# A pruned-weight matmul: PSUM banks shared by two tiles, and the first weights loaded in two parts

## The chip, the cores and the metric

One core of a Trainium2 chip. The metric is the device time of one execution in microseconds (us); lower is better. A timed execution is some 1.8 us longer than the span in its profile.

## The reference, cut to what matters

```python
B, S, D = 16, 512, 1024                       # x [16,512,1024], w [1024,1024], b [1024], all bf16
wg = w.reshape(D // 4, 4, D)                  # groups of four rows
mag = jnp.abs(wg)
thr = second largest of mag along axis 1
wp = (wg * (mag >= thr)).reshape(D, D)        # 2:4 pruning
return jnp.einsum("bsd,df->bsf", x, wp) + b
```

So: 8192 rows of x against a 1024 x 1024 matrix that must first be pruned, in groups of four rows. The matmul is nearly all of the time; what can be lost is the time until pruned weights and transposed x are there.

## The kernel before

The rows of w are laid out so that a partition holds the four rows of a group side by side. w is pruned in **pieces**: 0 to 3 are columns 0-256, 256-512, 512-768 and 768-1024 of the first half of the rows, 4 and 5 are the second half in 512 columns. While VectorE prunes, TensorE works on the first eight **tiles** of x (128 rows each): it transposes them, and multiplies each piece as soon as it is ready ("M6.0y" is tile 6, piece 0, the last two rows of each group). The sums lie in six PSUM banks; ScalarE evicts them ("S"), and GpSimd adds the bias later.

```python
load_w(0, 0, 256)               # SyncE's queue: piece 0, 256 KB
load_x(7, 8, "act")             # ScalarE's queue: x of tile 7
load_x(5, 7)                    # SyncE again: x of tiles 5 and 6, and so on
load_x(0, 2)
load_w(0, 256, 512)             # piece 1
load_x(2, 4)
load_x(4, 5)
load_w(0, 512, 1024)            # pieces 2 and 3, 512 KB
# ... (cut)
def mm_piece(t, i, ms):         # one tile, one piece
    g, c0, c1 = pieces[i]
    h = c0 // FH                # FH = 512: a bank holds ONE tile, two pieces
    # ... (cut)
order = {                       # each engine's instructions in program order (cut)
  "pe":  "T7a F2 T5a T6a F6 T0a T1a F6 M6.0x M5.0x ... M3.1y M2.2 M4.2 ...",
  "dve": "abs0 lo0 hi0 t20 t10 thr0 mask0x mult0x mask0y abs1 mult0y ... thr2 lo3 mask2 mult2 ...",
  "act": "C7a C5a C6a C0a C1a C2a C4a abs2 abs3 S6h0 C3a S5h0 ...",
}
```

T is a transpose, C its copy to SBUF, F a filler matmul on zeros that keeps TensorE busy while it has no data.

Of the kernel before, what the change touches and what calls it, by code (L numbers as in the profile page):

```python
# [10 lines left out]
def kernel(  # L11
# [7 lines left out]
    nc = tc.nc  # L19
    P = 128  # L20
# [12 lines left out]
    FH = 512  # L33
# [6 lines left out]
    NPK = 8  # L40
    LEAD = 4
    GROUPS = ((0, 5), (5, 8))
    LATE = 8
    sizes = (4, 8, 8, 8, 8, 8, 8)
    batches = []
    t0 = NPK + LEAD
# [29 lines left out]
    def act(i):  # L76
        return seq("act", i)
# [20 lines left out]
    def issue(eng, out_, in_):  # L98
        q = nc.sync if eng == "sp" else nc.scalar
        return seq(eng, q.dma_start(out_, in_))  # L100

    def load_w(g, c0, c1, eng="sp"):
        issue(eng, w_sb[:, g, :, c0:c1], wv[:, g, :, c0:c1])

    def load_x(ta, tb, eng="sp"):
        xs = const.tile([P, tb - ta, HK], bf16, name=f"x_{ta}")
# [2 lines left out]
        for t in range(ta, tb):  # L109
            x_sb[t] = xs[:, t - ta, :]  # L110

    load_w(0, 0, 256)
    load_x(7, 8, "act")
    act(nc.scalar.activation(spark[:], zeros[:, :1], Act.Abs))
    load_x(5, 7)
    load_x(0, 2)
    load_w(0, 256, 512)
    load_x(2, 4)
    load_x(4, 5)
    load_w(0, 512, 1024)  # L120
    load_w(1, 0, 512)
    sp(nc.sync.dma_start(bias_sb[:], b.partition_broadcast(P)))
# [19 lines left out]
    class Piece:  # L142
# [12 lines left out]
        def abs_act(self):  # L155
            act(nc.scalar.activation(self.mag[:], self.w, Act.Abs))  # L156

        def do(self, step, ms):
            magv = self.mag[:].rearrange("p (a j) f -> p a j f", j=2)
            hi, lo, thr = self.hi, self.lo, self.hi[:, 0, :]  # L160
            n = ms.stop - ms.start
            if step == "abs":
                dve(nc.vector.tensor_single_scalar(  # L163
                    self.mag[:].bitcast(u16), self.w.bitcast(u16), 0x7FFF, op=Alu.bitwise_and))
            elif step == "hi":
                self.tt(hi[:], magv[:, :, 0, :], magv[:, :, 1, :], Alu.max)
            elif step == "lo":
                self.tt(lo[:], magv[:, :, 0, :], magv[:, :, 1, :], Alu.min)
            elif step == "t1":
                self.tt(hi[:, 0, :], hi[:, 0, :], hi[:, 1, :], Alu.min)  # L170
            elif step == "t2":
                self.tt(lo[:, 0, :], lo[:, 0, :], lo[:, 1, :], Alu.max)
            elif step == "thr":
                self.tt(thr, hi[:, 0, :], lo[:, 0, :], Alu.max)
            elif step == "mask":
                self.tt(self.mag[:, ms, :], self.mag[:, ms, :],
                        thr[:, None, :].to_broadcast([P, n, self.n]), Alu.is_ge)
            else:
                self.tt(wp[:, self.g, ms, self.c0:self.c1], self.w[:, ms, :], self.mag[:, ms, :], Alu.mult)
# [14 lines left out]
        xpk[t] = xt  # L194

    ps_open = {}
    part = {"": slice(0, 4), "x": slice(0, 2), "y": slice(2, 4)}
    left = {}

    def mm_piece(t, i, ms):  # L200
        g, c0, c1 = pieces[i]
        h = c0 // FH
        new = (t, h) not in ps_open
        if new:
            ps_open[(t, h)] = psum_o.tile([P, FH], fp32, name="ps")
            left[(t, h)] = sum(4 for pc in pieces if pc[0] == 0 and pc[1] // FH == h)
        ps = ps_open[(t, h)]
        for m in range(ms.start, ms.stop):
            left[(t, h)] -= 1
            pe(nc.tensor.matmul(ps[:, c0 - h * FH:c1 - h * FH], lhsT=xpk[t][:, m, :],  # L210
                                rhs=wp[:, g, m, c0:c1],
                                start=(new and m == ms.start), stop=(left[(t, h)] == 0),
                                skip_group_check=True))

    xlead = const.tile([P, KT, LEAD * P], bf16)
# [27 lines left out]

    staged = {}

    def stage(t, h):
        st = stg.tile([P, FH], fp32, name=f"st{h}")
        act(nc.scalar.copy(st[:], ps_open.pop((t, h))[:]))  # L248
        staged[(t, h)] = st

    order = {
        "pe": (
            "T7a F2 T5a T6a F6 T0a T1a F6 M6.0x M5.0x M0.0x M7.0x M1.0x M1.0y M6.0y M5.0y T2a M0.0y "
            "T4a M7.0y T3a M2.0x M2.0y M6.1y M5.1y M2.1y M7.1y M0.1x M6.1x M5.1x M1.1y M0.1y M2.1x "
            "M7.1x M1.1x M4.0x M4.1x M4.0y M4.1y M3.0x M3.1x M3.0y M3.1y M2.2 M4.2 M7.2 M6.2 M3.2 "
            "M1.2 M2.3 M6.3 M7.3 M3.3 M5.2 M4.3 A3h0 M1.3 M0.3 A2h0 A3h1 A1h0 M0.2 M5.3 A0h0 A1h1 "
            "A2h1 A0h1"
        ),
        "dve": (
            "abs0 lo0 hi0 t20 t10 thr0 mask0x mult0x mask0y abs1 mult0y hi1 lo1 t11 t21 thr1 mask1y "  # L260
            "mult1y mask1x mult1x lo2 hi2 t22 t12 thr2 lo3 mask2 mult2 hi3 t13 t23 thr3 mask3 mult3 "
            "abs4 hi4 lo4 t14 t24 thr4 mask4 mult4 abs5 hi5 lo5 t25 t15 thr5 mask5 mult5"
        ),
        "act": (
            "C7a C5a C6a C0a C1a C2a C4a abs2 abs3 S6h0 C3a S5h0 S0h0 S7h0 S1h0 S2h0 S4h0 S3h0 S2h1 "
            "S6h1 S7h1 S4h1 S1h1 S3h1 S0h1 S5h1"
        ),
        "sp": (
            "W0.0 X0 W0.1 X1 W1.0 Y1 W1.1 Y0"
# [3 lines left out]
    p = {}  # L273
    halves = {0: ('x', 'y'), 1: ('x', 'y')}

    def all_of(tok, i):
        return [tok + x for x in halves.get(i, ("",))]

    def split_tok(tok):
        k = tok[-1] if tok[-1] in "xy" else ""  # L280
        return (tok[:-1] if k else tok), k

    transposed = []
# [1 line left out]
    def needs(eng, tok):  # L285
        base, k = split_tok(tok)
        if tok[0] == "C":
            return ["T" + tok[1:]]
        if tok[0] == "T":
            return ["C" + transposed[-2]] if len(transposed) > 1 else []  # L290
        if tok[0] == "F":
            return []
        if tok[0] == "W":
            g, h = map(int, tok[1:].split("."))
            return [n for i, pc in enumerate(pieces) if pc[0] == g and pc[1] // FH == h for n in all_of(f"mult{i}", i)]
        if tok[0] in "XY":
            return []
        if tok[0] == "A":
            return ["X0", f"W0.{tok.split('h')[1]}"]
        if base[0] == "M":  # L300
            t, i = base[1:].split(".")
            return [f"C{t}a", f"mult{i}{k}"]
        if tok[0] == "S":
            t, h = tok[1:].split("h")
            return [f"M{t}.{n}" for i, pc in enumerate(pieces) if pc[0] == 0 and pc[1] // FH == int(h)
                    for n in all_of(str(i), i)]
        i, step = base[-1], base[:-1]
        before = {"abs": [], "hi": ["abs"], "lo": ["abs"], "t1": ["hi"], "t2": ["lo"],
                  "thr": ["t1", "t2"], "mask": ["thr", "hi", "lo"], "mult": ["mask"]}[step]
        return [b_ + i + (k if b_ == "mask" else "") for b_ in before]  # L310

    def emit(eng, tok):
        base, k = split_tok(tok)
        if tok[0] == "T":
            transpose(int(tok[1:-1]))
            transposed.append(tok[1:])
        elif tok[0] == "F":
            filler(int(tok[1:]))
        elif tok[0] == "W":
            g, h = map(int, tok[1:].split("."))  # L320
            spread(g, h * FH, (h + 1) * FH)
        elif tok[0] == "X":
            xnat.update(load_lead(int(tok[1:])))
        elif tok[0] == "Y":
            xnat.update(load_low(int(tok[1:])))
        elif tok[0] == "A":
            open_nat(*map(int, tok[1:].split("h")))
        elif tok[0] == "C":
            copy_xt(int(tok[1:-1]))
        elif tok[0] == "M":  # L330
            mm_piece(*map(int, base[1:].split(".")), part[k])
        elif tok[0] == "S":
            stage(*map(int, tok[1:].split("h")))
        else:
            i = int(base[-1])
            if i not in p:
                p[i] = Piece(i)
            if eng == "act":
                p[i].abs_act()
            else:  # L340
                p[i].do(base[:-1], part[k])

    def run(queues):
        while any(queues.values()):
# [24 lines left out]

    pruned = const.tile([P, 1], bf16)  # L370
    pool(nc.gpsimd.tensor_copy(out=pruned[:], in_=wp[:, 1, 3, Dout - 1:]))
    closes = [(8, 0), (9, 0), (10, 0), (11, 0), (5, 0), (6, 0), (7, 0), (8, 1), (9, 1), (10, 1), (11, 1), (5, 1), (6, 1), (7, 1), (0, 0), (0, 1), (1, 0), (1, 1), (2, 0), (2, 1), (3, 0), (3, 1), (4, 0), (4, 1)]
    for t, h in closes:
        if t < NPK:
            pool(nc.gpsimd.tensor_tensor(staged[(t, h)][:], staged[(t, h)][:], bias_sb[:, h * FH:(h + 1) * FH], op=Alu.add))  # L375

    def evac(o, ps, c0, c1, add=None):
        dve(nc.vector.tensor_tensor(o[:, c0:c1], ps, bias_sb[:, c0:c1] if add is None else add, op=Alu.add))  # L378

    def rows(t):  # L380
        if t < NPK:
# [10 lines left out]
    def close(t, h):  # L392
# [3 lines left out]
        if ps is None:  # L396
            ps = psum_o.tile([P, FH], fp32, name="ps")
        nat(xnat[t], ps[:], h * FH, (h + 1) * FH, 4, 8, first=4 if t < NPK else 0, koff=4 if t < NPK else 0)
        add = staged.pop((t, h))[:] if t < NPK else None
        evac(outs[t], ps[:], h * FH, (h + 1) * FH, add)  # L400
        closed[t] = closed.get(t, 0) + 1
        if closed[t] == 2:
# [61 lines left out]
```

## Time and profile before

| | before |
|---|---|
| median of the first three runs | 233.93 us (233.49 to 234.32) |
| the profiled execution | 234.54 us, span 232.7 us |
| first matmul of piece 0 | 7.08 us |
| TensorE waits for an eviction | 0.71 us, until 13.89 |
| first matmul of piece 2 | 15.62 us |
| last bias add on VectorE starts | 230.11 us |

The table is read against TensorE, which is 98% busy: a gain is real only if TensorE reaches its last, unbroken stretch earlier. The lines are shown in the prediction below.

### The profile page before, as it was taken

What the parts mean: (1) busy time and instruction counts of PE and PEld (TensorE: products, weight loads), DVE (VectorE), ACT (ScalarE), POOL (GpSimd) and SP (SyncE); (2) the same over time, 40 slices, a digit from 0 to 9 for tenths busy, and PEclk for the clock granted to TensorE, in tenths of its full rate; (3) what the DMA queues carried; (4) which work ended last, traced back from release to release, by engine and by line L of the source; (5) the groups of instructions that cost most, each with busy time, mean ns of one, the idle gap of its engine ahead of it and who ended that gap; (6) DMA issues with size and microseconds to landing.
All of it is one profiled execution on the core that took longest, in us unless ns stands there. A gap on an engine that the chain in (4) does not pass through costs nothing.

```text
span 232.7 us, 2873 instructions
## 1 busy us (share of the span) xinstructions
PE 227.9 (98%) x1164; PEld 112.5 (48%) x1164; DVE 107.5 (46%) x181; ACT 14.4 (6%) x28; POOL 18.7 (8%) x23
## 2 busy tenths in 40 slices
PE   8989999999999999999999999999999999999995
PEld 4877544554444444444444444444444444444443
DVE  3889968763244244234334334324324424423434
ACT  4395200000000000000000000000000000000000
POOL 1000099910000000000000000000000000000000
PEclk9999999999999999999999999999999999999999
DMA  6996989998489611992239921696228951122122
GB/s 192 337 222 143 171 186 172 367 303 255 187 177 218 195 64 71 217 267 105 90 91 221 274 93 45 139 251 197 93 90 165 252 172 65 70 90 90 49 89 90
DMA packets 78652, 38.19 MB, mean 164 GB/s; under 512 B 63664, under 2 KB 71344, under 8 KB 78640
## 3 DMA queue, kind: packets, MB, share of 16 engines
q1 hardware_dynamic: 68128, 21.27, 46.0%
q10 hardware_dynamic: 10512, 16.75, 20.0%
q8 instruction: 9, 0.15, 0.3%
q14 instruction: 3, 0.02, 0.1%
HBM read 3.41 MB, written 16.78 MB: 87 GB/s over the span
## 4 chain that ended last, share of the span: by engine, by line
PE 93%; DMA 3%; SPq 1%; ACT 1%; issue 0%; DVE 0%
PE ps L233 88%; PE ps L210 4%; DMA w_sb<-in_w_dram 3%; PE tp L233 1%; SPq L100 1%; ACT mag L156 1%; ACT st L248 0%; DVE o L378 0%
## 5 line engine op out<-in xcount | busy, mean ns | idle before, releaser
L233 PE MATMUL ps<-wp_nat,xb 128*128 128x512 bf16 (+2 forms) x848 | 179.8, 375 | 0.0
L233 PEld LDWEIGHTS <-xb 128*128 128x128 bf16 x848 | 82.4, 98 | 97.5
L378 DVE TENSOR_TENSOR o<-ps,bias_sb 128x512 bf16<-128x512 f32 (+1 forms) x112 | 71.6, 677 | 113.6 <-PE ps L233 113.5
L375 POOL TENSOR_TENSOR st<-st,bias_sb 128x512 f32<-128x512 f32 x16 | 17.9, 1158 | 0.0
L210 PE MATMUL ps<-wp,xt 128*128 128x256 bf16 x128 | 15.2, 272 | 0.7 <-ACT st L248 0.7
L233 PE MATMUL ps<-wp_nat,xlow 128*128 128x512 bf16 x64 | 14.1, 379 | 0.0
L210 PEld LDWEIGHTS <-xt 128*128 128x128 bf16 x128 | 12.2, 98 | 2.8 <-issue 0.9
L378 DVE TENSOR_TENSOR o<-ps,st 128x512 bf16<-128x512 f32 x16 | 11.1, 692 | 2.9 <-PE ps L233 2.7
L233 PE MATMUL ps<-wp_nat,xlead 128*128 128x512 bf16 x48 | 11.0, 379 | 0.0
L233 PEld LDWEIGHTS <-xlow 128*128 128x128 bf16 x64 | 7.2, 112 | 6.7
L233 PEld LDWEIGHTS <-xlead 128*128 128x128 bf16 x64 | 6.3, 98 | 6.9
L248 ACT COPY st<-ps 128x512 f32<-128x512 f32 x16 | 8.4, 605 | 5.1 <-PE ps L210 5.1
L132 PE MATMUL ps<-zeros 128*128 128x128 bf16 (+1 forms) x28 | 4.8, 331 | 1.0 <-DVE zeros L86 1.0
L153 DVE TENSOR_TENSOR wp<-w_sb,mag 128x512 bf16<-128x512 bf16 (+2 forms) x8 | 5.5, 691 | 0.2
L153 DVE TENSOR_TENSOR mag<-mag,hi 128x512 bf16<-128x512 bf16 (+2 forms) x8 | 5.5, 689 | 0.2
L233 PE MATMUL tp<-wp_nat,xlead 128*128 128x512 bf16 x16 | 4.1, 379 | 0.0
L132 PEld LDWEIGHTS <-zeros 128*128 128x128 bf16 x28 | 2.6, 120 | 2.7 <-issue 1.7
L153 DVE TENSOR_TENSOR lo<-mag 128x512 bf16<-128x512 bf16 (+1 forms) x6 | 3.1, 510 | 1.3 <-ACT mag L156 1.3
L163 DVE TENSOR_SCALAR mag<-w_sb 128x1024 uint16<-128x1024 uint16 (+1 forms) x4 | 2.2, 556 | 3.1 <-DMA w_sb<-in_w_dram 3.1
L188 PE MATMUL tp<-ident,x 128*128 128x128 bf16 x32 | 2.9, 220 | 0.5 <-DMA x<-in_x_dram 0.3
L193 ACT COPY xt<-tp 128x256 f32<-128x256 f32 x8 | 2.8, 374 | 5.0 <-PE tp L188 4.7
L153 DVE TENSOR_TENSOR hi<-mag 128x512 bf16<-128x512 bf16 (+1 forms) x6 | 3.1, 509 | 0.1
(16 smaller groups left out, 14.4 us busy)
## 6 DMA issues: line engine op xcount, KB each, us to landing
out_dram<-o ACTq DMA_DIRECT2D x56, 256.0 KB, 2.7
wp_nat<-wp SPq DMA_DIRECT2D x16, 128.0 KB, 2.8
out_dram<-o ACTq DMA_DIRECT2D x14, 128.0 KB, 1.7
w_sb<-in_w_dram SPq DMA_DIRECT2D x3, 512.0 KB, 7.8
x<-in_x_dram SPq DMA_DIRECT2D x3, 256.0 KB, 4.1
w_sb<-in_w_dram SPq DMA_DIRECT2D x2, 256.0 KB, 3.8
bias_sb<-in_b_dram SPq DMA_DIRECT2D x1, 256.0 KB, 7.8
x<-in_x_dram ACTq DMA_DIRECT2D x1, 128.0 KB, 2.3
```

Source lines behind the costliest of these rows:

```text
L100: return seq(eng, q.dma_start(out_, in_))
L132: pe(nc.tensor.matmul(warm_ps[:, :rep * P], lhsT=zeros[:], rhs=zeros[:, None, :].to_broadcast([P, rep, P]), start=True, stop=True))
L153: dve(nc.vector.tensor_tensor(out, a, b_, op=op))
L156: act(nc.scalar.activation(self.mag[:], self.w, Act.Abs))
L163: dve(nc.vector.tensor_single_scalar(self.mag[:].bitcast(u16), self.w.bitcast(u16), 0x7FFF, op=Alu.bitwise_and))
L188: pe(nc.tensor.transpose(tp[:, m, :], xg[:, m, :], ident[:]))
L193: act(nc.scalar.copy(xt[:].bitcast(fp32), xpk[t].bitcast(fp32)))
L210: pe(nc.tensor.matmul(ps[:, c0 - h * FH:c1 - h * FH], lhsT=xpk[t][:, m, :], rhs=wp[:, g, m, c0:c1], start=(new and m == ms.start), stop=(l ...
L233: pe(nc.tensor.matmul(ps, lhsT=xt[:, kt - koff, :], rhs=wp_nat[:, kt, c0:c1], start=(kt == first), stop=(kt == last)))
L248: act(nc.scalar.copy(st[:], ps_open.pop((t, h))[:]))
L375: pool(nc.gpsimd.tensor_tensor(staged[(t, h)][:], staged[(t, h)][:], bias_sb[:, h * FH:(h + 1) * FH], op=Alu.add))
L378: dve(nc.vector.tensor_tensor(o[:, c0:c1], ps, bias_sb[:, c0:c1] if add is None else add, op=Alu.add))
```

## The change

Two parts that have nothing to do with each other. **Banks:** a bank now holds 256 columns of two tiles instead of 512 columns of one, so it is full, and can be evicted, as soon as one piece is done. **First weights:** piece 0 comes in two loads, the first two rows of each group and the last two, and VectorE starts on the first half. All orders were re-arranged with it, and the loads of x of tile 4 and of tiles 2 and 3 changed places; one more store of the output stays whole (LATE is 7 for 8).

```diff
-    load_w(0, 0, 256)
+    load_w(0, 0, 256, 0, 2)
     load_x(7, 8, "act")
+    load_w(0, 0, 256, 2, 4)
     load_x(5, 7)
     load_x(0, 2)
     load_w(0, 256, 512)
+    load_x(4, 5)
     load_x(2, 4)
-    load_x(4, 5)
...
-        h = c0 // FH
-        new = (t, h) not in ps_open
+        q, n = pair_of[t], c0 // CW              # pairs (5,6) (0,1) (2,3) (7,4), CW = 256
+        new = (q, n) not in ps_open
...
-  "pe":  T7a F2 T5a T6a F6 T0a T1a F6 M6.0x M5.0x ...
+  "pe":  T7a F2 T6a T5a F8 T1a T0a M6.0y M5.0y M7.0y M1.0y M6.0x M5.0x M1.0x T4a M0.0y T2a ...
-  "dve": abs0 lo0 hi0 t20 t10 thr0 ...            thr2 lo3 mask2 mult2
+  "dve": abs0a hi0a abs0b lo0a hi0b lo0b t10 t20 thr0 ...   thr2 mask2 mult2 lo3
-  "act": ... C4a abs2 abs3 S6h0 C3a ...
+  "act": ... C2a S0b0 C3a abs2 S3b0 abs3 ...
...
-    pool: 16 bias adds of 128x512
+    pool: 8 bias adds of 128x1024 (bias broadcast over the two tiles)
```

## The prediction

> **What bounds the kernel now.** I read the page first, then the chain of waits in order of time, then the timelines of TensorE and VectorE up to 45 us.
>
> ```profile
> span 232.7 us, 2873 instructions
> ...
> PE 227.9 (98%) x1164; PEld 112.5 (48%) x1164; DVE 107.5 (46%) x181; ACT 14.4 (6%) x28; POOL 18.7 (8%) x23
> ```
>
> TensorE is busy for 98% of the span, so the change can only win from what is not matmul. The chain says where that is:
>
> ```profile
> 4.41 6.93 DMA w_sb<-in_w_dram
> 11.34 0.02 issue
> 11.37 2.00 ACT mag L156 x2
> 13.37 0.48 ACT st L248
> 13.85 0.04 issue
> 13.89 7.19 PE ps L210 x64
> ...
> 39.24 190.85 PE ps L233 x900
> ```
>
> Columns are start, length and what ran. Up to 13.9 us the end is set by a load of weights, two absolute values on ScalarE and one eviction; from 13.9 us on it is TensorE without a hole. The last stretch gives the true rate: 190.85/900 = 0.212 us per matmul (a few are narrower than 512 columns; four full ones take 0.86 in the chain, so 0.216 each, and a 256-wide one 0.108). Nothing after 39 us is touched, apart from one store that stays whole (LATE 8 to 7). So the time moves only by what moves TensorE's progress before that.
>
> ```profile
> 6.27 0.64 PE L188 MATMUL tp<-ident,x 128*128 128x128 bf16 x8 [0.34 <-DMA x<-in_x_dram]
> 6.74 0.50 PE L132 MATMUL ps<-zeros 128*128 128x128 bf16 x6
> 7.08 1.91 PE L210 MATMUL ps<-wp,xt 128*128 128x256 bf16 x16
> ...
> 9.93 3.26 PE L210 MATMUL ps<-wp,xt 128*128 128x256 bf16 x28
> 13.89 7.19 PE L210 MATMUL ps<-wp,xt 128*128 128x256 bf16 x64 [0.71 <-ACT st L248]
> ```
>
> The 28 matmuls from 9.93 need 28 x 0.108 = 3.02, so TensorE really stood from 12.95 to 13.89: 0.94 us. The seventh bank was wanted (tile 4, after 5, 6, 0, 7, 1, 2), the first eviction ran only at 13.3 because ScalarE did both absolute values before it. This is the wait that sharing banks is to remove. But ask what comes next. The 64 matmuls from 13.89 begin with the last 16 of pieces 0 and 1 (1.73 us, to 15.62); the 17th is the first of piece 2, and VectorE closes that piece at 14.92 + 0.69 = 15.61:
>
> ```profile
> 12.46 0.43 DVE L153 TENSOR_TENSOR lo<-mag 128x512 bf16<-128x512 bf16 x1 [1.31 <-ACT mag L156]
> ...
> 13.86 0.42 DVE L153 TENSOR_TENSOR lo<-mag 128x512 bf16<-128x512 bf16 x1
> 14.20 0.69 DVE L153 TENSOR_TENSOR mag<-mag,hi 128x1024 bf16<-128x1024 bf16 x1
> 14.92 0.69 DVE L153 TENSOR_TENSOR wp<-w_sb,mag 128x1024 bf16<-128x1024 bf16 x1
> ```
>
> Two limits meet within 0.01 us at 15.6. **The bank wait is almost free today:** had it not been there, TensorE would have stood as long for piece 2's weights. Behind piece 2 stand the load that lands at 11.34, one absolute value on ScalarE (1.05) and seven instructions on VectorE. That is the real bound of the opening.
>
> **What the Trainium skill says.** "PSUM — Partial Sum Buffer", The four PSUM rules: a matmul with the first flag clears the marks of a whole 2 KiB bank, and later groups in disjoint columns that lack the flag find them clear and overwrite. The new code sets the flag only on a bank's first matmul, so two tiles in one bank should be right; the kernel before already puts two pieces of a tile in one bank. [...] the 128 KB of x takes 2.3 us from issue to landing, the first 256 KB of weights 3.0. "VectorE: DVE Perf Modes", The TRN2 errata: a fixed cost per instruction. Here 256 elements take 284 ns, 512 take 422 and 1024 take 690: about 0.15 us fixed, so cutting an operation into halves costs time on VectorE. "TensorE: Matmul & The Clock Gate", Part 1: an idle window of about 3.4 us lowers the clock; the stop of 0.94 us here did not (0.108 per matmul on both sides), and the ones I foresee are as short.
>
> **Part 1, first weights in two loads.** The 256 KB load lands at 3.8 and VectorE starts there. Issues take 0.46 to 0.68 us each on SyncE, so the half is issued from 0.73 to about 1.35 and the second to about 1.95. Estimate: the first half lands 0.45 us earlier (128 KB at the some 300 GB/s of the second slice), at 3.3, the second still near 3.8. Absolute value and first max of half a then run ahead of 3.8. From there, with starts apart by 0.2 (independent, 256 elements) and 0.32 (dependent), as the rows before show (4.94 to 5.14, 5.14 to 5.46): abs b 3.8, lo a 4.0, hi b 4.2, lo b 4.4, t1 4.6, t2 4.85, threshold 5.15, mask 5.5, mult 5.95, done 6.4. Today done is 6.68, so 0.3 us earlier. But the first matmuls now stand behind the transposes of tiles 1 and 0, whose x lands at 6.26: 8 x 0.055 = 0.43 more, 6.7. Today they start at 7.08, held by six fillers; the new order puts the fillers before the transposes. **First matmul 0.4 us earlier.**
>
> **Part 2, banks by pair and piece.** The same 16 evictions of 128x512 (605 ns each) and the same 128 matmuls. From 6.7: the 32 of piece 0 (3.46) and 12 transposes (0.65) end at 10.8; piece 1's halves, begun at some 7.3 behind the landing of its load, are done at about 10.2 and 11.0, each before its matmuls come. Then 32 of piece 1: 14.2. One new bank wait: the eighth bank asked for (tiles 5 and 6, piece 1) is the one that tiles 7 and 4 had, evicted after the first absolute value, at 12.4 + 0.57 = 13.0, and wanted at 12.7. So **TensorE is ready for piece 2 at about 14.5**, 1.1 us earlier than now.
>
> **Part 3, piece 2's weights.** Their load carries the same bytes ahead of it. Its issue slips by one issue, 0.5 us, but it waits in a backlog (DMA 0.98 busy from 5 to 10 us; 6.93 us from issue to landing), so I take the landing as unchanged, perhaps 0.1 earlier. The new VectorE order takes one lo of piece 3 (0.34 between starts, 13.86 to 14.20) out from before piece 2's mask, 0.2 after the dependent gap: lo 12.46, mask 13.98, mult 14.70, done 15.39. So the first matmul of piece 2 goes at 15.4 instead of 15.62. **Gain 0.2; a stand of about 0.9 us for the weights takes the place of the bank wait.**
>
> **Part 4, afterwards.** Piece 2 is now all 32 matmuls, to 18.85; piece 3 on VectorE gets an absolute value of piece 4 (0.61) put in before its mask: mult 18.2, done 18.9. Lost 0.05. Piece 3 is followed by the same work as now; its spread goes out at 18.9 rather than 18.28 (four issues of 0.62, 2.8 to landing: 23.6), wanted at about 24.4. VectorE is continuous from 12.46 to 29.5 and its work there is the same, so pieces 4 and 5 are ready as now; the spread of piece 5 lands at about 34.3, wanted at 35.4. Fits, with 1 us.
>
> **Part 5, bias adds on GpSimd.** 16 of 1158 ns become 8 of twice the size: 8 x 2.3 = 18.5 us from 29.7, ending at 48.2; the last is wanted at about 48.4, with six banks (5 us) of slack before TensorE feels it. No change.
>
> **The sum.** Part 1's 0.4 and part 2's 0.94 are on the way to 14.5 but not to 15.4; what reaches the end is part 3 less part 4, some 0.2, with perhaps 0.1 from an earlier start of the transfers: 0.3 of 233.93, **233.6 us**.
>
> **Rivals.**
> (a) The whole bank wait is won: about 1 us, 232.9. For it speaks that the chain names it; against it, piece 2's end at 15.61. It needs piece 2's load to land a microsecond earlier with the same bytes ahead of it.
> (b) The additional issue delays the loads: every SyncE issue after the first slips by 0.5. If the landing at 11.34 slips as much, piece 2 is ready at 15.9 and the time is 234.2. The backlog speaks against it.
> (c) GpSimd becomes the bound: if the broadcast bias makes an add half as dear again (3.5 us), the last ends at 57.5, 9 us late, 4 more than the banks hold: 238, slower by 2%. Its operands keep contiguous runs of 256, so I give it a few per cent.
> (d) The split loads are hidden anyway: x of tiles 0 and 1 lands at 6.26 whatever the weights do. I hold this to be so: the two loads alone are worth nothing at the end.
>
> **Range and chances.** The three times before spread by 0.8 us (233.49 to 234.32), about what a shift of one landing would give. From (a) and (b): 232.9 to 234.2. Faster by 2% needs 4.7 us, while all idle time of TensorE is 4.8 us, of which 1.0 at the start and 2.6 at the end are out of reach: 0.01. Slower by 2% needs (c) or a broken order: 0.02.
>
> **What would show it.** Right: first matmul at about 6.7; no wait on an eviction over 0.4 us; instead a wait of TensorE on VectorE's last multiply for piece 2, 0.7 to 1.1 us, ending near 15.4; a start of the last long stretch 0.1 to 0.4 us earlier. GpSimd adds at about 2.3 us each, ending before 49. Wrong: a landing of piece 2's load far from 11.3; a hole in TensorE after 19 us from a spread that lands late; adds over 2.6 us; or no wait on VectorE at 15, which would mean that I misread the order.

## The result, and the profile after

The changed kernel took 234.38 us (median of 4, 233.99 to 234.45) beside 234.12 us (233.49 to 234.35) for the kernel before. Executions over 1.5% slower than the fastest of the same kernel are left out of the means. A ratio here is the mean time of one kernel's runs over that of the other's of the same rounds, so not quite the ratio of the medians: 1.0012, 95% interval 0.9988 to 1.0036. So it is the same within noise; the forecast of 233.6 and its range to 234.2 were missed on the high side. Later batches did not tell the two apart either (1.0006 and 1.0008, below). Over all batches, the medians are 234.04 us (42 runs of before) and 234.09 us (16 of the changed kernel).

The chain of waits of the changed kernel, in order of time (start, length, what ran):

```profile
4.12 5.64 DMA x<-in_x_dram
9.76 0.05 issue
9.81 0.41 PE tp L189 x4
10.22 0.44 PE ps L215 x4
10.66 0.22 PE tp L189 x4
10.88 10.48 PE ps L215 x96
```

No eviction, no absolute value and no weights are in it any more. The load that sets the end is x of tiles 2 and 3: issued at 4.12, landed at 9.76. TensorE's timeline shows the hole:

```profile
6.47 0.64 PE L189 MATMUL tp<-ident,x 128*128 128x128 bf16 x8
6.95 1.69 PE L215 MATMUL ps<-wp,xt 128*128 128x256 bf16 x14
8.47 0.39 PE L189 MATMUL tp<-ident,x 128*128 128x128 bf16 x4
8.70 0.38 PE L215 MATMUL ps<-wp,xt 128*128 128x256 bf16 x2
9.81 0.41 PE L189 MATMUL tp<-ident,x 128*128 128x128 bf16 x4 [0.73 <-DMA x<-in_x_dram]
10.06 0.60 PE L215 MATMUL ps<-wp,xt 128*128 128x256 bf16 x4
10.49 0.39 PE L189 MATMUL tp<-ident,x 128*128 128x128 bf16 x4
10.72 10.64 PE L215 MATMUL ps<-wp,xt 128*128 128x256 bf16 x96
```

The transposes of tiles 1 and 0 begin at 6.47 (6.27 before) and the first matmul at 6.95 (7.08 before): 0.13 us won, where 0.4 was foreseen. Then TensorE stands for x. From 10.72 on, 96 matmuls run without a stop: the bank wait is gone, and so is any wait for piece 2. The first matmul of piece 2 is the 45th of them, at 10.72 + 44 x 0.108 = 15.47.

On VectorE, the first weights:

```profile
3.39 0.29 DVE L164 TENSOR_SCALAR mag<-w_sb 128x512 uint16<-128x512 uint16 x1 [2.46 <-DMA w_sb<-in_w_dram]
...
4.12 0.29 DVE L164 TENSOR_SCALAR mag<-w_sb 128x512 uint16<-128x512 uint16 x1
...
6.25 0.42 DVE L154 TENSOR_TENSOR wp<-w_sb,mag 128x512 bf16<-128x512 bf16 x1
```

The first half was there at 3.39, but the second only at 4.12, later than the whole load of before (3.80). The first multiply ends at 6.67, just as before (6.68). **In this profile the two loads won nothing on their own path**; in the two later ones of the same kernel the multiply ends at 6.48 and 6.56, so 0.1 to 0.2 us were won. And they cost something elsewhere: the transfers of the whole core between 3 and 4 us, before and after (the last two columns are the DMA share and GB/s):

```profile
3.00:4.00 1.00, 1.00 (x7) 0.62 (x6) 0.20 (x1) 0.00 (x0) 0.00 (x0) 1.00 1.06 326
```

```profile
3.00:4.00 1.00, 1.00 (x7) 0.63 (x6) 0.57 (x2) 0.00 (x0) 0.00 (x0) 1.00 0.74 206
```

About 120 KB less were moved in that microsecond. By the trace's completion records, x of tiles 5 and 6 landed at 5.30 instead of 4.62. Behind it the delay shrinks: x of tiles 0 and 1 landed at 6.4 instead of 6.2, and the load of pieces 2 and 3 at 11.2 instead of 11.3. GpSimd's adds were no trouble:

```profile
L394 POOL TENSOR_TENSOR st<-st,bias_sb 128x1024 f32<-128x1024 f32 x8 | 16.7, 2128 | 0.0
```

### The profile page after: what moved, and what is told of

It reads as the page before. It is cut to its first block, busy times and chain, and to the rows that moved or that the text cites. A ratio compares the mean times of both kernels' runs of the same rounds, so it can differ in the third digit from the quotient of the medians.

```text
span 232.6 us, 2831 instructions
## 1 busy us (share of the span) xinstructions
PE 226.9 (98%) x1140; PEld 112.6 (48%) x1160; DVE 107.5 (46%) x184; ACT 14.5 (6%) x28; POOL 17.6 (8%) x15
## 4 chain that ended last, share of the span: by engine, by line
PE 94%; DMA 2%; SPq 1%; issue 1%; DVE 0%
PE ps L238 87%; PE ps L215 5%; DMA x<-in_x_dram 2%; PE tp L238 1%; SPq L100 1%; PE tp L189 0%; DVE o L398 0%
## 5 line engine op out<-in xcount | busy, mean ns | idle before, releaser
L238 PE MATMUL ps<-wp_nat,xb 128*128 128x512 bf16 (+1 forms) x831 | 178.9, 375 | 0.9
L394 POOL TENSOR_TENSOR st<-st,bias_sb 128x1024 f32<-128x1024 f32 x8 | 16.7, 2128 | 0.0
L215 PE MATMUL ps<-wp,xt 128*128 128x256 bf16 x128 | 15.1, 273 | 0.0
L154 DVE TENSOR_TENSOR lo<-mag 128x512 bf16<-128x512 bf16 (+2 forms) x7 | 3.2, 458 | 1.3 <-ACT mag L157 1.3
L164 DVE TENSOR_SCALAR mag<-w_sb 128x512 uint16<-128x512 uint16 (+2 forms) x5 | 2.4, 476 | 2.6 <-DMA w_sb<-in_w_dram 2.5
L154 DVE TENSOR_TENSOR hi<-mag 128x512 bf16<-128x512 bf16 (+2 forms) x7 | 3.2, 459 | 0.1
L189 PEld LDWEIGHTS <-x 128*128 128x128 bf16 x32 | 2.4, 120 | 1.6 <-DMA x<-in_x_dram 1.6
```

Source lines behind the costliest of these rows:

```text
L154: dve(nc.vector.tensor_tensor(out, a, b_, op=op))
L164: dve(nc.vector.tensor_single_scalar(self.mag[:, ms, :].bitcast(u16), self.w[:, ms, :].bitcast(u16), 0x7FFF, op=Alu.bitwise_and))
L189: pe(nc.tensor.transpose(tp[:, m, :], xg[:, m, :], ident[:]))
L215: pe(nc.tensor.matmul(ps[:, c0 + d:c1 + d], lhsT=xpk[t][:, m, :], rhs=wp[:, g, m, c0:c1], start=(new and m == ms.start), stop=(left[(q, n) ...
L238: pe(nc.tensor.matmul(ps, lhsT=xt[:, kt - koff, :], rhs=wp_nat[:, kt, c0:c1], start=(kt == first), stop=(kt == last)))
L394: pool(nc.gpsimd.tensor_tensor(st[:], st[:], bias[:, :, None, :].to_broadcast([P, 2, 2, CW]), op=Alu.add))
```

## The experiments

Theory: the bank wait stood beside piece 2's weights and was worth little alone; the two first loads leave a hole in SyncE's queue, make x late, and give back what the banks and orders win. Rivals: the miss is only scatter; the bank wait was the bound; the re-ordered loads are to blame. In each of the four batches, all kernels of a batch shared one chip.

**The kernel before again.** No edit.

> The kernel before, unchanged, run as an experiment of its own. Theory A (the prediction's 0.3 us was worked out from one slow execution: the profiled run of before took 234.54 us while its timed median was 233.93): times spread over 233.5 to 234.5 and a second profile shows TensorE's start of piece 2 (the 17th matmul after its wait) elsewhere than 15.62, since the landing of piece 2's load jitters. Rival B (the spread comes from the end or from outside the span): the start of the last long stretch stays at 39.07 within 0.05 us and only the time outside it differs.

234.26 us, ratio 1.0003 (0.9986 to 1.0020). Its own second profile (234.77 us) starts piece 2 at about the same place, 15.6, but TensorE then stands 0.16 us longer at 30.5 for a spread of pruned weights, and its last add starts at 230.36 rather than 230.11. So both A and B are partly wrong: times do spread by 1 us for one kernel, and part of it comes from single landings, but not from the one I named.

**The changed kernel again.** No edit, twice on different chips.

> The changed kernel, unchanged, beside before on one chip. If the changed kernel is really the same: ratio 0.998 to 1.002. If the loss of 0.26 us in the medians is real: 1.001 or more with an interval that leaves out 1. A second profile tells whether the stand of TensorE for x of tiles 2 and 3 at 9.1 to 9.8 us is there each time (theory: yes, 0.5 to 1.2 us) or was one slow landing (rival: under 0.2 us).

> The changed kernel unchanged, on the chip of this batch, to be set beside the other three. Theory: 233.8 to 234.4; a stand for x of 0.7 us or more in its profile once more, at tiles 5 and 6 or at 2 and 3; 0.3 us or more slower than the one-load kernel with halves.

1.0006 (0.9974 to 1.0038), median 233.80, and 1.0008 (0.9983 to 1.0033), median 234.25. The second was also to be 0.3 us or more slower than the one-load kernel with halves (below) in its batch, and was: 234.25 beside 233.77. In both profiles TensorE stands for x again, but now for the load before: x of tiles 5 and 6 landed at 6.12 and 6.47. The first of them:

```profile
6.14 0.64 PE L189 MATMUL tp<-ident,x 128*128 128x128 bf16 x8 [1.28 <-DMA x<-in_x_dram]
6.62 0.61 PE L133 MATMUL ps<-zeros 128*128 128x128 bf16 x8
7.07 0.62 PE L189 MATMUL tp<-ident,x 128*128 128x128 bf16 x8
7.53 1.69 PE L215 MATMUL ps<-wp,xt 128*128 128x256 bf16 x14
```

The first matmul is at 7.53 here and at 7.88 in the other, later than before's 7.08. In three of three profiles, then, the changed kernel loses 0.7 to 1.3 us to x, at one of two places. For x of tiles 2 and 3 at 9.76 the hole is not shown to be the cause: in the other two profiles this load landed at 8.7 and 9.0, in time.

**Before, with the first eviction between the two absolute values.**

```diff
-  "act": ... C4a abs2 abs3 S6h0 C3a ...
+  "act": ... C4a abs2 S6h0 abs3 C3a ...
```

> The kernel before with one token moved on ScalarE: the first eviction between the two absolute values instead of after them. Theory (the bank wait is almost free, since piece 2's weights come at 15.6 anyway): the wait on the eviction falls from 0.7 to 0.2 us or less, a wait on VectorE's multiply of piece 2 comes in its place, time within 0.2 us of before (ratio 0.999 to 1.001). Rival (the bank wait was the bound): 0.7 us faster, ratio 0.997.

Ratio 1.0019 (1.0002 to 1.0035): no gain, if anything a small loss that the theory did not expect. The wait on an eviction fell from 0.71 to 0.23:

```profile
14.27 6.46 PE L210 MATMUL ps<-wp,xt 128*128 128x256 bf16 x56 [0.23 <-ACT st L248]
```

and TensorE's weight load then waited 0.3 us for VectorE's multiply. The rival, that the bank wait was the bound and 0.7 us were to be had by removing it, falls. Its profile does start piece 2 some 0.3 us earlier (that of before was an execution with a later landing); the timed runs do not show it.

**The changed kernel, with x of tiles 2 and 3 ahead of piece 1.**

```diff
     load_x(0, 2)
+    load_x(2, 4)
     load_w(0, 256, 512)
     load_x(4, 5)
-    load_x(2, 4)
```

> The changed kernel with the load of x of tiles 2 and 3 put ahead of piece 1's weights. Theory: the stand of 0.9 us at the transposes of tile 2 goes; TensorE then reaches piece 2 at 14.6 and waits there for its weights until 15.3, so only 0.15 us is won (ratio to the changed kernel 0.999); piece 1's weights land 0.5 us later and may cost up to 0.3 of it. Rival (the stand for x is the bound): 0.8 us faster than the changed kernel, about 233.6 or less.

Ratio to before 1.0029 (1.0003 to 1.0054): if anything slower. The stand at the transposes of tile 2 is gone, but x of tiles 5 and 6 landed at 6.43, TensorE stood 1.62 us for it, and the first matmul came at 7.83. I had treated one load as the culprit; the order further back does not cure what happens ahead of it.

**The changed kernel, with the first weights in one load and pruned as before.**

```diff
-    load_w(0, 0, 256, 0, 2)
+    load_w(0, 0, 256)
-    load_w(0, 0, 256, 2, 4)
-  "dve": abs0a hi0a abs0b lo0a hi0b lo0b t10 t20 ...
+  "dve": abs0 lo0 hi0 t20 t10 ...
```

> The changed kernel with the first weights in one load again and pruned as before (banks, orders of TensorE and ScalarE kept). Theory (the second load of the first weights pushes x of tiles 5 and 6 from second to third on its queue and leaves a hole in the transfers at 3.3 to 4.3 us): x of 5 and 6 lands at 4.5 to 4.9 as in all three profiles with one load (changed kernel: 5.3, 6.1, 6.4), the 0.25 us slices from 3.5 to 4.25 carry 60 to 90 KB again, first matmul of piece 0 at about 6.75, and TensorE now waits 0.5 to 0.9 us for piece 2's weights; time equal to the changed kernel or up to 0.3 us faster. Rival (the hole has another cause, such as the reordered loads): x of 5 and 6 lands at 5.3 or later here too.

233.75 us beside 234.04: ratio 0.9988 (0.9969 to 1.0007). x of tiles 5 and 6 landed at 4.78, and 3 to 4 us carried 292 GB/s, as expected; the first matmul came at 7.19, later than the 6.75 expected. TensorE from the transposes of tiles 1 and 0 on:

```profile
6.72 0.64 PE L188 MATMUL tp<-ident,x 128*128 128x128 bf16 x8 [0.42 <-DMA x<-in_x_dram]
7.19 1.69 PE L214 MATMUL ps<-wp,xt 128*128 128x256 bf16 x14
...
10.04 10.64 PE L214 MATMUL ps<-wp,xt 128*128 128x256 bf16 x96
```

Piece 2 begins at 10.04 + 44 x 0.108 = 14.79. The expected wait for piece 2's weights did not come: their last multiply ended at 14.65. By the medians the banks and orders without the two loads are about 0.3 us to the good, which is what was predicted for the whole change; this run alone does not show it, since the interval includes 1.

**Before, with only the first load cut in two.**

```diff
-    load_w(0, 0, 256)
+    load_w(0, 0, 256, 0, 2)
     load_x(7, 8, "act")
+    load_w(0, 0, 256, 2, 4)
```

> The kernel before with only the first weights' load cut in two; pruning and everything else as before. Theory: the hole at 3.3 to 4.3 us appears, x of tiles 5 and 6 lands at 5.2 or later instead of 4.6, the first absolute value starts at about 4.1 instead of 3.8; 0.2 to 0.6 us slower. Rival (the cut is harmless): landings as in before, same time.

The hole appears in the old kernel too:

```profile
3.00:4.00 1.00, 1.00 (x7) 0.63 (x6) 0.04 (x1) 0.00 (x0) 0.00 (x0) 1.00 0.85 190
```

x of tiles 5 and 6 landed at 6.23, TensorE stood 1.0 us for it, and the first matmul moved from 7.08 to 7.96. But the time hardly did: 234.21 us, ratio 1.0010 (0.9991 to 1.0029), and the expected loss of 0.2 to 0.6 us is not shown. TensorE was late by as much as it would otherwise have stood for the bank and for piece 2; both of those waits are gone from this profile. The slack that makes the bank wait nearly free makes this loss nearly free.

**The changed kernel, with the second half issued by ScalarE.**

```diff
     load_x(7, 8, "act")
+    load_w(0, 0, 256, 2, 4, "act")
-    load_w(0, 0, 256, 2, 4)
```

> The changed kernel with the second half of the first weights issued by ScalarE, after its load of x, so that x of tiles 5 and 6 is second on SyncE's queue again. If the place on the queue makes the hole: x of 5 and 6 lands before 5.0, no hole. If the number of transfers in flight makes it: hole and late landing stay. Time within 0.4 us of the changed kernel; second half of the weights at about 3.8 to 4.1.

```profile
3.00:4.00 1.00, 1.00 (x7) 0.62 (x6) 0.48 (x2) 0.18 (x1) 0.00 (x0) 1.00 1.08 354
```

The same bytes in the same two halves, and no hole: x of tiles 5 and 6 at 4.83, the second half at 4.46 (later than expected, and later than the 3.8 to 4.1 with both on one queue), first matmul at 7.07. 233.83 us, ratio 0.9990 (0.9970 to 1.0009).

**One load, and the load of pieces 2 and 3 cut in halves.** On top of the one-load kernel:

```diff
-    load_w(0, 512, 1024)
+    load_w(0, 512, 768)
+    load_w(0, 768, 1024)
```

> The one-load kernel of this batch with the 512 KB load of pieces 2 and 3 cut into one of 256 KB for each. Theory (with one load the start is free and TensorE waits for piece 2's weights): piece 2 lands 0.5 to 1.2 us earlier, its last multiply ends at 14.2 to 14.8, TensorE's wait there falls under 0.3 us: 0.5 us faster than before (233.6). Rival (512 B runs in place of 1 KB cost as much as the cut wins, or another wait follows): same time as the one-load kernel.

> The one-load kernel with pieces 2 and 3 in halves, unchanged, on the chip of this batch. Theory: 233.3 to 233.7, faster than before by 0.4 to 0.8 us with an interval that leaves out 1. Rival (the 233.42 was luck): within 0.2 us of before.

233.42 us beside 234.04 (ratio 0.9980, 0.9959 to 1.0001), and 233.77 beside 233.94 in the next batch (0.9982, 0.9964 to 1.0000). By the ratios this is 0.4 to 0.5 us faster than before, at the edge of what these runs can show: the second was to give an interval that leaves out 1, and it ends at 1.0000. Since the one-load kernel alone had 233.75, the halves themselves are not shown to be worth anything: it never waited for piece 2.

**Before, with only pieces 2 and 3 in halves.** The same two lines in the old kernel.

> The kernel before, banks and orders untouched, with only the 512 KB load of pieces 2 and 3 cut into one of 256 KB for each. Theory (piece 2's weights were the bound of the opening and the bank wait stood beside them): the first absolute value starts at about 10.3 instead of 11.0 to 11.4, the eviction behind it follows, TensorE's wait on the eviction falls under 0.2 us and piece 2 begins at 14.6 to 15.0 instead of 15.62; 0.4 to 0.8 us faster than before. Rival (the bank layout is what counts): the wait on the eviction stays over 0.4 us and the time is that of before.

A miss: ratio 0.9997 (0.9979 to 1.0015). The wait on the eviction went away as expected and piece 2's last multiply ended at 14.77, yet TensorE came to piece 2 only after the 44 matmuls of pieces 0 and 1 that were left, at 10.50 + 44 x 0.108 = 15.25, later than the 14.6 to 15.0 expected:

```profile
10.50 10.21 PE L211 MATMUL ps<-wp,xt 128*128 128x256 bf16 x92
```

This execution started late (x of tiles 5 and 6 at 5.31, first matmul at 7.65, behind its second set of fillers); why, with one load, is not settled. So this profile does start piece 2 some 0.4 us before that of the kernel before, as the one with the early eviction does, but the timed runs show no gain from earlier weights alone in the old order.

**The halves on two queues, pieces 2 and 3 in halves.** The changed kernel, with ScalarE issuing the second half first:

```diff
+    load_w(0, 0, 256, 2, 4, "act")
     load_x(7, 8, "act")
-    load_w(0, 0, 256, 2, 4)
-    load_w(0, 512, 1024)
+    load_w(0, 512, 768)
+    load_w(0, 768, 1024)
```

> The changed kernel with the second half of the first weights issued by ScalarE ahead of its x, and the load of pieces 2 and 3 in halves. Theory: both halves land by 3.6, the last multiply of the first half of piece 0 ends near 6.2, the first matmul goes at 6.3 to 6.7 behind x of tiles 0 and 1; no wait over 0.3 us afterwards; 233.2 to 233.6, at or below the one-load kernel with halves. Rival (x of tile 7, now behind, or VectorE's later pieces take it back): no faster than that kernel.

233.61 us, ratio 0.9982 (0.9962 to 1.0002); 363 GB/s between 3 and 4 us. With both halves in time, the first multiply ended at 6.37, the earliest of all 16 profiles (the changed kernel 6.48 to 6.67, before 6.68). But x of tile 7, now second on ScalarE's queue, let the first transposes begin only at 4.79 (4.36 before), and with the fillers and transposes behind them the first matmul came at 7.00. Halving the weights does what it was meant for only when both halves come early (with the second half behind x of tile 7 it avoided the hole too, but the multiply ended at 7.01), and then TensorE's own way there is the limit: no better than one load.

**What makes the hole.** Two looks, each beside one run of before (234.88 us):

```diff
# before, an unused 4 KB load ahead of everything
+    tiny = const.tile([P, 16], bf16)
+    issue("sp", tiny[:], wv[:, 0, 0, :16])
     load_w(0, 0, 256)
```

> The kernel before with an unused 4 KB load put ahead of the first weights on SyncE's queue. If the place on the queue counts: x of tiles 5 and 6, now third, lands at 5.5 or later (4.6 before) and the transfers carry under 210 GB/s between 3 and 4 us. If the bytes and the timing of the two halves count: every landing slips by the 0.5 us of one issue, x of 5 and 6 to 5.1 or so, with no hole after the weights: over 260 GB/s from 3 to 4 us.

```diff
# the changed kernel, x of tiles 5 and 6 on ScalarE's queue
     load_x(7, 8, "act")
+    load_x(5, 7, "act")
-    load_x(5, 7)
```

> The changed kernel with x of tiles 5 and 6 issued by ScalarE behind its x of tile 7; both halves of the weights stay on SyncE's queue. If the place counts: x of 5 and 6, second on its queue, lands before 4.9, over 260 GB/s from 3 to 4 us, and x of tiles 0 and 1, now third on SyncE's, is the late one (after 6.0). If the two halves themselves make the hole: under 210 GB/s from 3 to 4 us here too.

In the first, x of tiles 5 and 6, now third, landed at 5.61 (the place says 5.5 or later), but 256 GB/s lies between the two forecasts, and the weights themselves slipped by 1.1 us with an issue only 0.45 us later: undecided. In the second there is no hole, as the place says:

```profile
3.00:4.00 1.00, 1.00 (x7) 0.63 (x6) 0.46 (x2) 0.17 (x1) 0.00 (x0) 1.00 1.21 351
```

x of tiles 0 and 1, now third on SyncE's queue, came at 6.62, after 6.0 as forecast; but it is third in the kernel before too, and came at 6.2 there, so this half of the forecast tells little. Over all 16 profiles, 3 to 4 us carried 131 to 206 GB/s in the five with both halves ahead of x of tiles 5 and 6 on SyncE's queue, and 256 to 363 in the eleven others. That the hole comes with both halves standing ahead of x on SyncE's queue, and goes when either one of them or x moves to the other queue, is shown. Place and issue time changed together, though: x of tiles 5 and 6 was issued at 1.75 in the five and at 1.2 to 1.5 in ten of the others (1.90 behind the 4 KB load). A delay of 0.28 us beside before does not account for a landing 0.7 to 1.8 us later, but which of the two starts it is not shown. In the five, the first of the 16 DMA engines reports this load at 4.4 to 4.7 us, hardly later than in before (4.2), and the last at 5.3 to 6.5 (4.6): some engines are late, not all. The mechanism stays open.

**What the hole costs.** In all 16 profiles the time of the execution is the start of piece 2's first matmul, read from the trace, plus 218.8 to 219.2 us. With the new banks and orders that start lies at 15.2 to 15.5 in the four profiles with the hole and at 14.5 to 15.0 in the six without it; the timed runs of these kernels have medians of 234.31 us (21 runs) and 233.64 us (30 runs, all on one chip, 18 of them with pieces 2 and 3 in halves as well). On that one chip, the batch that has both gives 234.25 beside 233.77 and 233.61. In the old order the start is at 15.3 to 15.7, and the hole makes no difference to be seen.

## Why the prediction was wrong

Point by point, in the order of the prediction:

- **What bounds the kernel now** held. The bank wait was nearly free: removing it alone gave no time (ratio 1.0019). That piece 2's weights were the real bound is not shown: earlier weights alone gave none either (0.9997).
- **Part 1 is the step that failed.** "The second still near 3.8": VectorE began on it at 4.12, 3.95 and 4.01 in the three profiles, and of its 0.3 us came 0.0, 0.2 and 0.1. "First matmul 0.4 us earlier" was 0.13 earlier in the first profile and 0.45 and 0.80 later in the other two. I costed the added transfer as one issue time on a backlog and asked only about its own landing. The issue time was even too dear: "every SyncE issue after the first slips by 0.5", but x of tiles 5 and 6 was issued 0.28 us later and piece 2 0.20. The runs show that it takes x of tiles 5 and 6 from 4.62 to 5.3-6.5 and leaves a hole of about 120 to 200 KB in the stream; that was in none of my terms, and with the new orders it moves piece 2's start from 14.5-15.0 to 15.2-15.5. Rival (b) had the idea but the wrong load, piece 2's.
- **Part 2** was right on the bank wait (gone in every profile), wrong on the way there: "TensorE is ready for piece 2 at about 14.5" took 12 transposes at 0.055 us each and no stop, where the changed kernel stood 0.7 to 1.3 us for x. With one load it was ready at 14.79.
- **Part 3**: piece 2 began at 15.47, 15.13 and 15.48, near the forecast 15.4, but for another reason. No "stand of about 0.9 us for the weights" came. In the second profile piece 2's load had landed at 10.5 by the completion records, and ScalarE's absolute value ran only at 10.93, straight behind its copy of tile 3. In the new order late x holds up the pruning of piece 2 as well, so TensorE and its weights slip together and no wait is seen. In nine of the ten profiles with the new order the absolute value starts 0.26 us after this copy does, and in the tenth 0.37; in the first and third of the changed kernel the load had also landed only just before, at 11.2. The second:

```profile
10.67 0.39 ACT L194 COPY xt<-tp 128x256 f32<-128x256 f32 x1
10.93 1.08 ACT L157 ACTIVATE mag<-w_sb 128x1024 bf16<-128x1024 bf16 x1
```

- **Part 4** held: no hole in TensorE after 19 us. **Part 5** held: 2.13 us an add against 2.3. Rivals (a) and (c) did not happen. Rival (d), that the two loads are worth nothing at the end, was my own view and was too kind to them.
- **The sum.** From one profile to the other, TensorE's end moved by 0.16 us (230.11 to 229.95) and the profiled executions from 234.54 to 234.37: close to the 0.2 to 0.3 worked out, but by luck: neither the wait for weights nor a start without a stop came. That difference I took off the median of three runs, 233.93, though it was read from an execution of 234.54. With time tied to piece 2's start as above, 15.62 was a late start for this kernel: its usual one is, as an estimate from 234.04 less 218.9, about 15.1, and the changed kernel's 15.1 to 15.5 is no gain on that. Of the miss against the pooled 234.09, about 0.1 is that base (pooled 234.04) and the rest the gain that does not show. The range also allowed too little for scatter: the runs of the kernel before go from 233.4 to 235.1, those of the changed one from 233.6 to 236.3.

## What to carry to other kernels

A small load added to a queue can be paid not by itself but by what stands behind it (here 0.7 to 1.8 us at the next load, for an issue 0.28 us later): ask which transfer it pushes back and who waits for that one, and try the other issuing queue before the same one. A wait named by the chain is worth only its distance to the next limit, so look for what would have stopped the engine a moment later; taking the wait away alone, or delaying the engine on purpose, shows that distance. And take a forecast's difference off many runs, not off three, when the difference is smaller than their spread; if it is read from one profile, see first whether that execution lies near the median (here it was 0.5 to 0.6 us above).

## What the Trainium skill lacked or had wrong

- "DMA: Bandwidth & Descriptors", Issuing engines are not separate DMA queues, says that issuing from several engines "will only save the time on the sequencer it takes to initiate the DMA". Here the same two halves moved 131 to 206 GB/s between 3 and 4 us when both went to SyncE's queue ahead of x, and 354 when the second was issued by ScalarE, with x of tiles 5 and 6 landing at 4.83 instead of 5.3 to 6.5. It was issued 0.50 us earlier (1.25 beside 1.75), so in four of the five looks more than issue time was saved; in the fifth (5.30) just that.
- No page has what short transfers in a row on one queue cost each other: 256 KB of x took 3.1 to 3.8 us from issue to landing in second place on SyncE's queue (nine looks) and 3.5 to 4.7 us in third behind the two halves (five looks), with the same bytes ahead of it; the ranges overlap.
- No page says how far apart the 16 engines of one transfer finish: for the 512 KB load of pieces 2 and 3 in the kernel before, the first engine reported at 8.7 us and the last at 11.4.
